# Attention and soft experts in one kernel: another order and pace for the loads of keys, values and expert weights

## The chip, the cores and the metric

The kernel runs on one core of a Trainium2 chip. Times are device microseconds of one execution. Three executions of the kernel before took 250.63, 252.06 and 254.31 us; their median, 252.06 us, is the time before. A fourth execution was taken by the hardware profiler and took 248.69 us; the profile that is quoted below is that one.

## The reference

The kernel computes windowed attention with a linear distance bias, and feeds its output as tokens into a soft mixture of experts. Cut to what matters:

```
# q, k, v: [8 batches, 8 heads, 576, 64]
scores = (q @ k^T) / 8
rel    = pos[:, None] - pos[None, :]
scores = where((rel >= 0) & (rel < 128), scores - slope[h] * |rel|, -1e9)
attn   = exp(scores - rowmax) / (rowsum + 1e-9)
x      = (attn @ v) as [4608 tokens, 512 features]

# phi: [512, 32 slots], w1: [8 experts, 512, 1024], w2: [8 experts, 1024, 512]
logits = x @ phi
d      = softmax of logits over the tokens      # dispatch
slot_input = d^T @ x                            # [32, 512], 4 slots an expert
slot_out[e] = relu(slot_input[e] @ w1[e]) @ w2[e]
c      = softmax of logits over the slots       # combine
out    = c @ slot_out                           # [4608, 512]
```

All inputs and the output are float32. Queries and keys carry a factor of 8, so the scores are well spread.

## The kernel before, in words

**Tiles.** A token tile is 128 queries of one batch with all eight heads. A batch has 576 = 4 x 128 + 64 tokens, so two batches make nine tiles: four of an even batch (t = 0 to 3), then five of the odd batch, whose last (t = 4) holds the two tails of 64 of both. There are 36 tiles, numbered k = 0 to 35; the last batch takes its tiles in the order 1, 2, 3, 4, 0. A tile has two halves (g = 0, 1) of 64 queries each.

**Keys** lie in memory by blocks of 64 keys, nine blocks (0 to 8) a batch, 128 KB each with all heads. They stay in SBUF in a ring of twelve blocks (`keys`, in the tile `kq`); `first_key` says where a batch starts. Half g of tile t reads three blocks from 2(t-1)+g on; t = 0 reads blocks 0 and 1 alone, and t = 4 reads blocks 6 to 8 of both batches. So tile 2 of a batch is the first to read block 5, tile 3 needs blocks 4 to 7, and block 8 is read by t = 4 alone.

**Queries** have two buffers (256 KB a tile, `load_q`); the load for tile k + 2 is asked for after tile k's scores. **Values** (264 KB a tile of 128 keys, `load_v`) have five buffers in the list `v_free`; the tails of two batches have a buffer of their own (`load_v_tails`, 264 KB).

**The pipeline** over k (lines 617 to 671) does, in one pass: VectorE merges the two halves of the window in the scores of tile k (`merge`, L274), adds the bias and takes the row maxima with their signs turned (`rowmax`, L283, into the small tile `nb`, of which there are two buffers, so half g of the next tile writes the buffer of half g of this one); ScalarE takes the exponentials (`expo`, L298); TensorE transposes tile k - 1's exponentials (`flip`, L316), ScalarE copies them to SBUF (`take`, L319), GpSimd cuts the window's corners (`split`, L336 and L339); TensorE forms tile k - 2's weighted values (`values`, L352, and `values_ex`, L364), then tile k + 1's scores (`scores`, L260); VectorE divides by the row sums (`x_store`, L375 to L378); tile k - 3's tokens are transposed (`x_flip`, L384) and copied (`x_keep`, L387). Every four tiles come the logits, the running dispatch maximum and sum, and `slot_sum` (L397 to L460). Each engine runs its instructions in the order in which this text issues them.

**Expert weights** come in 64 units of 512 KB (`units`): 32 of `w1`, then 32 of `w2`. The first NW = 35 go to a ring of 35 tiles; the next 16 go into buffers that the attention no longer needs (`place`: first the keys' and queries' tile, then values, then work areas); the last 13 reuse the ring after the first expert matmuls have read it.

**The pace of the weights.** All of these loads are issued by SyncE (SP), one after another, and each waits on SP until its buffer is free. To keep the units from being asked for too soon, `hold` (L144) first issues a transfer of four bytes from `nb` to a scratch row `beat`: SP cannot issue it before VectorE has written `nb`, and the unit stands behind it. In the text below this transfer is called a note. Before the change, tiles 3 to 29 have one note and one unit each, tiles 30 to 33 one note and two units; the tiles n - 3 = 33 and n - 2 = 34 ask for two more units each after the next tile's scores, and one is asked for after the loop. From there on the units are asked for in the same order with the last steps of the attention.

**The order at the start.** SP asks for key blocks 0 and 1, a small constant, key blocks 2 and 3, value 0, `phi` and a constant; ScalarE's queue asks for query 0, constants and query 1. `loads(0)`, called after tile 0's scores, asks for query 2, value 1 and key blocks 4 and 5; `loads(k)` goes on in that way, and `after_values(k)` loads values into the buffers that tile k was the last to read.

## Time and profile before

| | before |
|---|---|
| median of 3 executions | 252.06 us (250.63 to 254.31) |
| profiled execution | 248.69 us |
| its span, first to last instruction | 247.0 us |
| mean granted TensorE clock | 0.985 |
| TensorE busy | 233.9 us, 95% |
| VectorE, ScalarE busy | 176.3 us, 166.2 us |
| moved by the DMA engines | 72.87 MB, mean 295 GB/s |

The pipeline over the 36 tiles takes the first 185 us or so, the experts and the output the rest. In the profile, a line such as `L260` is a line of the kernel; `SPq` and `ACTq` are the queues of SyncE and ScalarE, on which loads are issued; the duration of an issue is the queue's own time, not the transfer's. In square brackets behind a row stands how long the engine was idle before it, and what ended that. The tile names are the program's: `kq` keys and queries, `va` values, `w` weights, `s` scores, `area` exponentials and their transposes, `nb` the turned maxima, `beat` the target of the notes.

### The profile page before, as it was taken

What the parts mean: (1) busy time and instruction counts of PE and PEld (TensorE: products, weight loads), DVE (VectorE), ACT (ScalarE), POOL (GpSimd) and SP (SyncE); (2) the same over time, 40 slices, a digit from 0 to 9 for tenths busy, and PEclk for the clock granted to TensorE, in tenths of its full rate; (3) what the DMA queues carried; (4) which work ended last, traced back from release to release, by engine and by line L of the source; (5) the groups of instructions that cost most, each with busy time, mean ns of one, the idle gap of its engine ahead of it and who ended that gap; (6) DMA issues with size and microseconds to landing.
All of it is one profiled execution on the core that took longest, in us unless ns stands there. A gap on an engine that the chain in (4) does not pass through costs nothing.

```text
span 247.0 us, 12332 instructions
## 1 busy us (share of the span) xinstructions
PE 233.9 (95%) x4867; PEld 176.4 (71%) x4869; DVE 176.3 (71%) x971; ACT 166.2 (67%) x474; POOL 94.7 (38%) x235
## 2 busy tenths in 40 slices
PE   7799999999999999999999999999998899999982
PEld 3488887877788778787788788788875433866640
DVE  1877878977998898798789899889876411244451
ACT  2778987969788888797797969868954110033441
POOL 2038355724642765086077507557550010000000
PEclk9999999999999999999999999999999999999985
DMA  6979987889889588798778789999878999977997
GB/s 172 305 244 320 302 246 218 248 300 309 241 252 308 178 284 271 248 353 272 253 225 259 258 234 362 354 343 338 293 249 282 416 401 411 409 308 312 353 374 298
DMA packets 28491, 72.87 MB, mean 295 GB/s; under 512 B 3344, under 2 KB 3858, under 8 KB 28434
## 3 DMA queue, kind: packets, MB, share of 16 engines
q1 hardware_dynamic: 27714, 71.25, 83.9%
q10 hardware_dynamic: 720, 0.84, 1.2%
q8 instruction: 38, 0.62, 1.0%
q14 instruction: 19, 0.16, 0.2%
HBM read 62.64 MB, written 9.44 MB: 292 GB/s over the span
## 4 chain that ended last, share of the span: by engine, by line
PE 50%; DVE 5%; issue 1%; ACT 1%; DVEq 0%
PE xp L352 7%; PE s L260 7%; PE op L803 6%; PE hp L767 6%; PE pt L316 5%; PE po L824 5%; PE xq L384 3%; PE xp L364 3%; PE ap L448 2%; PE lp L397 2%; DVE sq L283 1%; DVE xs L378 1%; PE dp L435 1%; DVE s L274 1%; PE ot L816 1%
## 5 line engine op out<-in xcount | busy, mean ns | idle before, releaser
L298 ACT ACTIVATE area<-sq,nb 128x128 f32<-128x128 f32 x288 | 89.5, 400 | 3.4 <-DVE nb L283 2.7
L339 POOL TENSOR_SCALAR_AFFINE_SELECT area<-area 64x256 f32<-64x256 f32 x112 | 46.2, 413 | 82.6 <-ACT area L319 73.9
L283 DVE CUSTOM_DVE_ANT_0 sq<-s,cst 128x128 f32<-128x128 f32 x224 | 51.8, 287 | 7.6
L319 ACT COPY area<-pt 128x512 f32<-128x512 f32 x71 | 41.9, 592 | 19.9 <-PE pt L316 18.4
L260 PE MATMUL s<-kq 64*64 64x192 f32 (+2 forms) x1152 | 51.7, 310 | 1.8 <-DMA kq<-k_t 1.4
L336 POOL TENSOR_SCALAR_AFFINE_SELECT area<-area 64x256 f32<-64x256 f32 x112 | 45.7, 418 | 5.8
L260 PEld LDWEIGHTS s<-kq 64*64 64x64 f32 x1152 | 40.0, 135 | 7.0 <-DVE nb L283 3.9
L316 PE MATMUL pt<-unit_r,area 128*128 128x128 f32 x288 | 44.3, 278 | 0.0
L352 PE MATMUL xp<-va,area 128*64 128x66 f32 x1120 | 40.8, 224 | 1.0 <-DVE xs L378 0.5
L352 PEld LDWEIGHTS xp<-va,area 128*64 128x64 f32 x1120 | 36.0, 137 | 7.0 <-issue 4.3
L316 PEld LDWEIGHTS pt<-unit_r,area 128*128 128x128 f32 x288 | 32.2, 141 | 7.1 <-ACT area L298 4.3
L274 DVE COPY_PREDICATED s<-cst,s 128x256 f32<-128x256 int32 (+1 forms) x73 | 30.6, 419 | 6.1 <-PE s L260 6.1
L378 DVE TENSOR_TENSOR xs<-xp,rs 128x256 f32<-128x256 f32 x70 | 26.5, 419 | 1.2
L387 ACT COPY xs<-xq 128x512 f32<-128x512 f32 (+1 forms) x36 | 21.0, 585 | 5.1 <-PE xq L384 4.8
L384 PE MATMUL xq<-unit_r,xs 128*128 128x128 f32 x144 | 22.5, 278 | 1.7 <-DVE xs L378 0.9
L283 DVE DVE_READ_ACCUMULATOR2_ANT nb<- 128x1 f32 x288 | 23.8, 83 | 0.0
L830 DVE COPY ob<-po 128x384 f32<-128x384 f32 x24 | 12.5, 554 | 13.8 <-PE po L824 13.2
L364 PEld LDWEIGHTS xp<-va,area 64*64 64x64 f32 x896 | 15.7, 133 | 7.5 <-issue 6.4
L830 ACT COPY ob<-po 128x384 f32<-128x384 f32 x24 | 10.5, 481 | 14.0 <-PE po L824 13.9
L364 PE MATMUL xp<-va,area 64*64 64x66 f32 x896 | 19.6, 224 | 0.0
L384 PEld LDWEIGHTS xq<-unit_r,xs 128*128 128x128 f32 x144 | 16.2, 141 | 4.1 <-PE pt L316 2.4
L283 DVE CUSTOM_DVE_ANT_0 sq<-s,fine 128x128 f32<-128x128 f32 x64 | 14.9, 287 | 1.9
(106 smaller groups left out, 230.1 us busy)
## 6 DMA issues: line engine op xcount, KB each, us to landing
w<-w SPq DMA_DIRECT2D x48, 512.0 KB
out<-ob SPq DMA_DIRECT2D x24, 384.0 KB
kq<-q_t SPq DMA_DIRECT2D x34, 256.0 KB
va<-v_n SPq DMA_DIRECT2D x32, 264.0 KB
kq<-k_t SPq DMA_DIRECT2D x24, 256.0 KB
kq<-k_t SPq DMA_DIRECT2D x8, 384.0 KB
kq<-w SPq DMA_DIRECT2D x4, 512.0 KB
area<-w SPq DMA_DIRECT2D x4, 512.0 KB
```

The source lines that it names most:

```text
L260: nc.tensor.matmul(parts[par][half[c], jh, KB * o:WIN], lhsT=qt[rows, j], rhs=keys[rows, i:i + 3 - o, j], start=(t > 0 and jh == 0), stop= ...
L274: nc.vector.copy_predicated(window(k, g, us, 0, KB), bc(mask_le, 1, len(range(4)[us])), window(k, g, us, P, KB))
L283: nc.vector.tensor_tensor_reduce(out=s["sq"][:, u], in0=window(k, g, u, 0, P), in1=bias[:, u] if tiles[k][1] else zero.to_broadcast([P, P] ...
L298: nc.scalar.activation(dst, s["sq"][:, u].rearrange("p (a w) -> p a w", a=2), AF.Exp, bias=s["nb"][:, u:u + 1], scale=-1.0)
L316: nc.tensor.transpose(s["pt"][:, u], s["p4"][:, u], ident)
L319: copy(pas[k % 2][:, g].rearrange("p a j m -> p (a j m)"), st[k, g]["pt"].rearrange("p u w -> p (u w)"))
L336: nc.gpsimd.affine_select(dst, pa, [[0, NPAIR], [-1, KB]], ALU.is_gt, 0.0, base=0, channel_multiplier=1)
L339: nc.gpsimd.affine_select(dst, pa, [[0, NPAIR], [1, KB]], ALU.is_ge, 0.0, base=0, channel_multiplier=-1)
L352: nc.tensor.matmul(x[par][half[g], j], lhsT=pas[k % 2][:, g, par, j], rhs=v[:, par, j], start=(j == 0), stop=(t == 0 and j == NPAIR - 1))
L364: nc.tensor.matmul(x[par][half[g], j], lhsT=pps[k % 2][rows, g, j], rhs=v, start=False, stop=(j == NPAIR - 1))
L378: nc.vector.tensor_tensor(x[:, par], xp[par][:, :, 0:D], bc(rs[:, par], 2, D), op=ALU.mult)
L384: nc.tensor.transpose(st["xq", k][:, P * j:P * j + P], xns[k % NXN][:, P * j:P * j + P], ident)
```

## The change

1. Key blocks 4 and 5 of the first batch are asked for ahead of value 0, not in `loads(0)`.
2. The notes and units start at tile 1 instead of tile 3, with one unit a tile through tile 33. Tiles 33, 34 and 35 ask for two, three and two more after the next tile's scores (in tile 35: after the values), in place of two, two and the one after the loop.
3. In the tiles 1, 2, 15, 28, 29, 30, 32 and 33 the note reads the maxima of the second half instead of the first.
4. Blocks 6 to 8 of a batch, one load of 384 KB at t = 1, become blocks 6 and 7 (256 KB) at t = 1 and block 8 of both batches (128 KB each) at t = 2 of the odd batch.
5. A tile asks for one value load at most: where two buffers come free at once (t = 4 of an odd batch), the second load follows one tile later. The value tails of two batches are asked for at the first tile of the odd batch instead of at t = 0 of the even one.

```diff
-WFIRST = 3
+WFIRST, WLAST = 1, NTT - 2
+TAIL_LOADS = {3: 2, 2: 3, 1: 2}
+LATE = (1, 2, 15, 28, 29, 30, 32, 33)
...
+        load_k(0, 4, 6)
         load_v()
         nc.sync.dma_start(phi, phid)
         nc.sync.dma_start(ends, seld)
...
-        if t == 0 and b < last:
+        if t == 0 and 0 < b < last:
             now.append(k_part(b, 4, 6))
         if t == 1:
-            now.append(k_part(b, 6, NB))
+            now.append(k_part(b, 6, NB - 1))
+        if b % 2 and t == 2:
+            now += [k_part(b - i, NB - 1, NB) for i in range(2)]
...
-        for _ in done:
+        if t or k == 0 or b % 2 == 0:
             load_v()
-        if t == 0 and b % 2 == 0:
+        if b % 2 and t == order(b)[0]:
             load_v_tails(b)
...
     def weights(k):
-        if k >= WFIRST and loaded[0] < NW:
-            hold(st[k, 0]["nb"])
+        if WFIRST <= k < WLAST:
+            hold(st[k, k in LATE]["nb"])
             load_weight()
-            if k >= n - 6:
-                load_weight()
...
+            chain(k, 1)
             weights(k)
-            chain(k, 1)
...
-            if k in (n - 3, n - 2):
-                load_weight()
+            for _ in range(TAIL_LOADS.get(n - k, 0)):
                 load_weight()
...
-        load_weight()
         nc.gpsimd.memset(inp, 0.0)
```

## The prediction

> **What bounds the kernel now.** I read the profile's page first, then the busy time by stretches of the span, then the list of who waited for whom, and last the order in time of TensorE, VectorE, ScalarE and the SyncE queue in the first 20 us. First the page and the stretches; after each pair of times stand its length, then the busy time of TensorE (PE), its weight loads, VectorE (DVE), ScalarE (ACT), GpSimd (POOL), then the granted clock, the busy share of the DMA engines and GB/s.

> ```profile
> span 247.0 us, 12332 instructions
> PE 233.9 (95%) x4867; PEld 176.4 (71%) x4869; DVE 176.3 (71%) x971; ACT 166.2 (67%) x474; POOL 94.7 (38%) x235
> ...
> 10.00:15.00 5.00, 3.61 (x56) 2.97 (x56) 3.49 (x25) 4.25 (x13) 0.00 (x0) 1.00 0.83 274
> 15.00:20.00 5.00, 4.49 (x89) 3.80 (x85) 4.45 (x31) 4.35 (x13) 3.62 (x9) 1.00 0.88 275
> 20.00:150.00 130.00, 128.65 (x2974) 106.17 (x2970) 110.92 (x657) 108.69 (x317) 66.30 (x162) 1.00 0.84 265
> 150.00:172.00 22.00, 21.79 (x511) 18.14 (x508) 19.06 (x112) 18.83 (x57) 14.95 (x37) 1.00 0.99 355
> 172.00:184.00 12.00, 11.52 (x273) 9.54 (x274) 10.30 (x55) 9.34 (x28) 7.38 (x19) 1.00 0.80 277
> 195.00:217.00 22.00, 22.00 (x320) 10.53 (x320) 4.11 (x18) 1.33 (x4) 0.95 (x3) 1.00 1.02 406
> ```

> TensorE sets the pace. From 20 to 172 us it is busy 150.44 of 152 us, so no change in the order of loads can win more than 1.56 us there; from 195 to 217 it never stops. Before the output stage the idle time that loads could have caused is therefore mostly the 1.39 us of 10 to 15 and the 0.51 us of 15 to 20. The transfers are uneven: 406 GB/s is the most that a stretch shows, 355 (share 0.99) is reached from 150 to 172, and 165 to 275 elsewhere.

> Next, single lines of the list of waits, each with the total, the count and the longest:

> ```profile
> PE s L260 <- DMA kq<-k_t: 1.4, 1, 1.4
> SPq L195 <- DMA kq<-q_t: 1.6, 1, 1.6
> SPq L195 <- PE xp L364: 21.2, 16, 2.4
> SPq L178 <- PE pt L316: 36.4, 25, 3.7
> ```

> Only one matmul in the whole span was held up over 1 us by a load: one score matmul by a key load. Every other entry that matters has SP waiting for TensorE, that is, loads waiting for buffers.

> **The change, part by part.** (1) *Key blocks 4 and 5 of the first batch* move from behind query 2 and value 1 to ahead of value 0. The rows below are TensorE around the wait, and SP's issues from the start.

> ```profile
> 9.77 1.09 PE L316 MATMUL pt<-unit_r,area 128*128 128x128 f32 x8
> 12.25 1.53 PE L260 MATMUL s<-kq 64*64 64x192 f32 x32 [1.39 <-DMA kq<-k_t]
> 13.71 1.09 PE L316 MATMUL pt<-unit_r,area 128*128 128x128 f32 x8
> 14.73 1.16 PE L352 MATMUL xp<-va,area 128*64 128x66 f32 x32
> 16.06 1.53 PE L260 MATMUL s<-kq 64*64 64x192 f32 x32 [0.17 <-DVE nb L283]
> ...
> 2.39 0.35 SPq L185 DMA_DIRECT2D kq<-k_t  x1
> 4.38 0.33 SPq L195 DMA_DIRECT2D va<-v_n  x1
> 7.50 0.33 SPq L178 DMA_DIRECT2D kq<-q_t  x1
> 7.87 0.43 SPq L195 DMA_DIRECT2D va<-v_n  x1
> 8.34 0.43 SPq L185 DMA_DIRECT2D kq<-k_t  x1
> 10.74 0.44 SPq L185 DMA_DIRECT2D kq<-k_t  x1
> ```

> The load asked for at 8.34 let tile 2's scores start at 12.25: 3.91 us. SP reached the value load at 4.38 only after 1.6 us of waiting for an earlier transfer (the wait list), so the key load in its place goes out at 4.38, not at 2.8. With 3.91 us it lands at 8.3; with the 5.7 us between the key load of 2.39 and the start of tile 1's scores, it lands at 10.1. Either is ahead of 10.86, when the transposes of 9.77 end. Next late is query 2, asked for at 7.50, now with 256 KB more ahead of it. It came two transfers (520 KB) before the key load that ended the wait.

> ```profile
> 10.00:12.00 2.00, 0.86 (x8) 0.63 (x6) 1.82 (x15) 1.87 (x6) 0.00 (x0) 1.00 1.01 333
> 12.00:14.00 2.00, 1.75 (x35) 1.50 (x36) 0.67 (x4) 1.54 (x5) 0.00 (x0) 1.00 0.87 301
> 14.00:16.00 2.00, 1.89 (x40) 1.59 (x38) 1.81 (x16) 1.84 (x6) 0.03 (x1) 1.00 0.54 165
> ```

> At 333 GB/s those 520 KB are 1.6 us, so query 2 was there by about 10.7; 256 KB more are 0.8 us, so 11.5 at the latest. Tile 2's scores then start at 10.86 to 11.5: 0.75 to 1.39 us earlier.

> That gain does not reach tile 2's end whole, because of ScalarE:

> ```profile
> 10.13 1.28 ACT L298 ACTIVATE area<-sq,nb 128x128 f32<-128x128 f32 x4 [0.55 <-DVE nb L283]
> 11.32 1.04 ACT L319 COPY area<-pt 128x512 f32<-128x512 f32 x2
> 12.26 1.28 ACT L298 ACTIVATE area<-sq,nb 128x128 f32<-128x128 f32 x4
> 14.15 1.28 ACT L298 ACTIVATE area<-sq,nb 128x128 f32<-128x128 f32 x4 [0.62 <-PE pt L316]
> ```

> It works without a break from 10.13 to 13.54 on tile 1, which the change does not touch. The second exponentials, ended at 13.54, release the last four of the eight transposes; now all eight begin at 13.71. With early scores the first four can run before that, and the last four start at 13.71 instead of 13.71 + 1.09 / 2 = 14.26. So 0.55 us remain: the weighted values come at 14.18 and tile 3's scores at 15.51. ScalarE's wait of 0.62 before 14.15 shrinks with it. Tile 3's scores need the load of 10.74: it was there by 16.06 with 384 KB, and is now 256 KB, 0.4 us less at 333 GB/s, so by 15.66 at worst. I take -0.5 us (ends 0 and -1.39; nearer to the ScalarE row, which holds whatever query 2 does). With TensorE full from 20 us on, it stays won to the end.

> (2) *Two more units of weights at the start.* Tiles 1 and 2 now each ask for 512 KB (tile 3 was the first), while 264 KB of value tails go to the next batch and 128 KB of keys to later. That is about 0.65 MB more between 12 and 18 us. From 14 to 16 alone, (406 - 165) GB/s x 2 us = 0.48 MB is free, and from 12 to 14 another 0.2. Cost 0; without that room 0.65 MB at 406 GB/s, 1.6 us, for loads that are used a tile and more later.

> (3) *One unit instead of two in tiles 30 to 33*, with two or three in tiles 33 to 35 after the scores. The stretch from 150 to 172 loses about two units (1 MB of its 7.8); 172 to 184 takes them, where (406 - 277) x 12 us = 1.5 MB is free. At the end of the last tile the count of units is 40 either way, so the saturated stretch from 195 on sees the same queue. TensorE does not wait for a load in either, so 0 in the profiled execution.

> (4) *Eight notes wait for the second maxima.* VectorE around tiles 1 and 2, and SP's first two notes:

> ```profile
> 11.24 0.08 DVE L283 DVE_READ_ACCUMULATOR2_ANT nb<- 128x1 f32 x1
> 13.19 0.43 DVE L274 COPY_PREDICATED s<-cst,s 128x256 f32<-128x256 int32 x1 [1.23 <-PE s L260]
> 14.61 0.42 DVE L274 COPY_PREDICATED s<-cst,s 128x256 f32<-128x256 int32 x1
> 15.39 0.08 DVE L283 DVE_READ_ACCUMULATOR2_ANT nb<- 128x1 f32 x1
> ...
> 19.04 0.66 SPq L144 DMA_DIRECT2D beat<-nb  x1
> 23.55 0.59 SPq L144 DMA_DIRECT2D beat<-nb  x1
> ```

> SP stands some 1.42 us longer there, the distance between the merges of 13.19 and 14.61, which open a tile's first and second maxima. Behind it on SP are the unit, the value load and the next query and key loads. Those value and query loads wait for TensorE anyway, 21.2 / 16 = 1.3 and 36.4 / 25 = 1.5 us each, and are used more than a tile later: 0; without this cover each would go out up to 1.4 us later.

> (5) *Key loads of 256 + 128 KB instead of 384, value tails later, one value load per tile.* Eight more issues of 0.43 us and two more notes of 0.59 on a queue that mostly waits: 0. The last key blocks are asked for two tiles, some 9 us, ahead of their scores, the tails three to four tiles ahead; against 3.9 to 5.7 us from issue to use that is enough.

> [...]

> Sum: 247.0 - 0.5 = 246.5 us of span. The profiled execution took 248.69 (1.69 around the span), so 248.2. The median of the runs, 252.06, is 3.37 above it; the same half microsecond off gives **251.6 us**.

> **The rivals.** *Late keys in the timed runs* (A). The runs are 3.37 us slower than the profiled execution, and something in them waits that the profile does not show. The best candidate is the stretch at share 0.99:

> ```profile
> 147.96 1.14 SPq L185 DMA_DIRECT2D kq<-k_t  x2
> 153.99 0.99 SPq L154 DMA_DIRECT2D w<-w  x2
> 159.05 0.89 SPq L154 DMA_DIRECT2D w<-w  x2
> ...
> 155.58 1.48 PE L260 MATMUL s<-kq 64*64 64x192 f32 x32
> ```

> Two key loads of 147.96 are used at 155.58, and double units stand ahead of later ones. If all 3.37 us are lost there, the change takes them back: 252.06 - 3.37 - 0.5 = 248.2. Against it: the profiled execution shows no wait there.

> *Nothing* (B). Query 2 or tile 3's keys come so late that tile 3's scores stay at 16.06, or the key load, which SP cannot issue before 4.38, queues longer than 5.7 us: 252.1.

> *The notes become a wait* (C), slower. A note reads the minima's buffer, and VectorE may not write that buffer again until the note has landed.

> Tile 1's note can go out at 11.3 (VectorE's rows above); its buffer is written again at 15.39, or 14.3 once the 1.23 us wait is gone: 3.0 us. A note's landing is in no row; the nearest is the 3.91 us key load, so up to 0.9 us of stall. For the notes of tiles 2 and 3, with a unit ahead (512 KB at 333 GB/s, 1.6 us), 5.5 us stand against a tile of 4.5: 1.0 us each. If TensorE follows all three, 2.9 - 0.5 = +2.4, 254.5. It decides from a landing of 3.0 us in tile 1 and 4.5 after. Against: notes at that pitch hold up nothing now, and ScalarE, which comes next, is busy with copies.

> *A fixed cost per transfer* (D). Of the 3.91 us, 256 KB at 406 GB/s are 0.65; if the other 3.3 us kept the engines from other work, eight more loads would cost 26 us: 278. Against: at 3.3 us each, 512 KB units would move at 114 GB/s, and they move at 406 from 195 to 217. [...]

> **How the numbers follow.** Forecast 0.50 (251.6), A 0.15 (248.2 to 251), B 0.20 (252.1), C 0.13 (252.3 to 254.5, seldom more), D 0.02. The range 249.1 to 253.6 leaves out the lower half of A, the upper half of C and D. What a measurement can tell from no change is about 2%, 5.0 us. No case but a full A with more behind it saves that: 0.02; D and a C that goes on past tile 3 lose it: 0.04; within: 0.94.

> **What would show it.** Tile 2's scores starting at 10.9 to 11.5 with a wait under 0.7, ended by a query load; the last transposes of tile 1 still at 13.7; tile 3's scores about 15.5, and everything to the end half a microsecond earlier. The stretch from 150 to 172 falls near 310 GB/s. VectorE waiting for a note in tiles 2 to 4 would be C; a score matmul waiting for keys after tile 3, or a weights wait after 195, would prove (2) or (3) wrong.

## The result and the profile after

| | before | after |
|---|---|---|
| median of 17 executions | 253.95 us (250.15 to 257.98) | 255.26 us (252.24 to 265.39) |
| profiled execution | 248.69 us | 254.91 us |
| its span | 247.0 us | 253.2 us |
| mean granted TensorE clock | 0.985 | 0.982 |

After over before is 1.0117, 95% interval 1.007 to 1.0164. So the change makes the kernel about one per cent slower: less than the 2% that the chances speak of, but slower, where the forecast was half a microsecond faster. The ratios here leave out executions more than 1.5% above the fastest of their kernel; two experiments get none for that reason, and only their median is given. The profiled execution of before, at 248.69 us, is below all 17 timed ones, so the 6.2 us between the two spans are more than the change costs on average.

The page of after, its first lines and the line of one DMA queue (packets, megabytes, share of the time of 16 engines), and the same line of before:

```profile
span 253.2 us, 12347 instructions
PE 234.6 (93%) x4867; PEld 176.7 (70%) x4869; DVE 176.4 (70%) x971; ACT 166.0 (66%) x474; POOL 94.7 (37%) x235
...
q8 instruction: 38, 0.62, 1.1%
```

```profile
q8 instruction: 38, 0.62, 1.0%
```

No engine has more to do than before. TensorE is busy 0.7 us longer, and the span is 6.2 us longer: TensorE stands idle. The stretches of after say where (the columns are those of the prediction):

```profile
20.00:150.00 130.00, 125.94 (x2904) 103.37 (x2900) 107.98 (x636) 105.21 (x307) 64.52 (x158) 1.00 0.85 264
150.00:172.00 22.00, 21.84 (x470) 17.86 (x464) 19.27 (x114) 18.45 (x54) 13.43 (x33) 1.00 0.87 275
172.00:184.00 12.00, 10.55 (x281) 9.21 (x277) 9.99 (x62) 10.79 (x34) 8.36 (x22) 1.00 0.88 293
184.00:195.00 11.00, 9.87 (x172) 7.51 (x176) 5.74 (x20) 3.58 (x9) 1.54 (x4) 0.84 0.84 283
```

From 20 to 150 us TensorE lost 2.71 us more than before (125.94 busy instead of 128.65), from 172 to 184 another 0.97, and from 184 to 195 the granted clock, 1.00 everywhere else here, is 0.84. The list of waits of after names what ended the idle time of the matmuls (total, count, longest):

```profile
PE xp L355 <- issue: 3.2, 2, 2.0
...
PE s L263 <- issue: 1.2, 1, 1.2
...
PE lp L400 <- issue: 0.4, 1, 0.4
```

"issue" is time in which an engine waits for nothing that the profile shows. In order of time, the three longest of these stands are:

```profile
22.93 0.81 PE L355 MATMUL xp<-va,area 128*64 128x66 f32 x20
24.93 0.57 PE L355 MATMUL xp<-va,area 128*64 128x66 f32 x12 [1.19 <-issue]
...
50.81 1.48 PE L263 MATMUL s<-kq 64*64 64x192 f32 x30
53.45 0.54 PE L263 MATMUL s<-kq 64*64 64x192 f32 x2 [1.15 <-issue]
...
181.64 0.92 PE L355 MATMUL xp<-va,area 128*64 128x66 f32 x23
184.56 0.51 PE L355 MATMUL xp<-va,area 128*64 128x66 f32 x9 [2.00 <-issue]
```

Each breaks a run of equal matmuls in the middle: 20 of 32 done, then nothing for 1.19 us, then the other 12. No wait for an operand is on record there. What was missing, by the measurements of the next part, is the instructions.

**How instructions come.** TensorE has 4867 matmuls, 4869 weight loads and some 133 instructions of its sequencer, 9869 in before. The queue marked "instruction", q8, carries 38 packets, each of 16384 bytes in the traces of before and after. Counted along TensorE's stream, every one of these stands lies just ahead of instruction 448 + 256 j: in after at 704, 1216, 1728, 1984, 4032 and 7872, in before at 1984 and 6848 (one or two later in kernels with as many sequencer instructions more). With 38 x 256 = 9728 I take one packet as a block of 256 TensorE instructions. A block's packet follows the moment at which TensorE starts on the block before it, which I call the request; that the packet is asked for there is my reading of the times. It starts 0.2 to 6.5 us behind the request in 477 of 480 blocks of the profiles of this study (in the other three up to 0.4 us ahead of it), lasts 0.9 to 2.8 us, mostly 1.0, and where TensorE has run dry it goes on 1.1 to 1.6 us after the packet's end. In the steady loop 256 instructions last about 5.1 us. So, by my estimate, a packet that starts over 5.1 - 1.0 - 1.4 = 2.7 us behind its request comes too late. From the packets and instructions of after, all in us:

```
request   packet starts      packet ends   TensorE goes on   stand
 19.00    22.64 (+3.64)       23.70         24.93             1.19
 30.02    33.45 (+3.43)       34.42         35.76             0.42
 41.82    44.72 (+2.90)       45.68         47.01             0.10
 47.01    51.02 (+4.01)       51.92         53.45             1.15
 93.11    95.01 (+1.91)       97.24         98.60             0.10
177.68   182.18 (+4.50)      183.14        184.56             2.00
```

**Where the 6.2 us went.** Compared instruction by instruction, after starts the 700th TensorE instruction 0.83 us earlier than before, and the 8200th (at 193.8 us in after) 6.09 us later. On the way it loses 1.36 us around the stand at 24.9, 0.73 at 35.8, 0.36 at 47.0, 0.86 at 53.4 (before has a stand of its own there), 0.45 at 98.6, wins back 0.08, and loses 3.24 around 184.6: -0.83 + 1.36 + 0.73 + 0.36 + 0.86 + 0.45 - 0.08 + 3.24 = 6.09. The losses around the first five stands come to 3.76, the stands themselves to 2.96; what the rest is made of I have not traced. In the last term 2.00 us are the stand itself; behind it the trace shows the granted clock at 0.5 from 186.0 for 3.4 us (1.00 from 184.0 to 186.0), in which eight transposes took 1.97 us, against 1.09 at 12.80; I estimate that this costs up to half of the 3.4, 1.7. The sums of the recorded stands are 4.96 us in after and 0.45 in before, whose two are at 158.9 (0.21) and here:

```profile
50.98 0.54 PE L260 MATMUL s<-kq 64*64 64x192 f32 x3 [0.24 <-issue]
```

**What the late packets have in common.** SP's queue in after, ahead of the requests of 19.00 and 177.68 (`w<-w`, and `kq<-w` late in the span, are units of 512 KB):

```profile
12.03 0.37 SPq L156 DMA_DIRECT2D w<-w  x1
...
15.75 0.38 SPq L156 DMA_DIRECT2D w<-w  x1
...
18.61 0.38 SPq L156 DMA_DIRECT2D w<-w  x1
...
173.29 0.38 SPq L156 DMA_DIRECT2D w<-w  x1
173.73 1.25 SPq L204 DMA_DIRECT2D va<-v_t  x1
175.02 0.91 SPq L156 DMA_DIRECT2D w<-w  x2
176.02 4.88 SPq L156 DMA_DIRECT2D kq<-w  x4
```

These are the places where the change puts units: three by 19.0, where before had its first at 19.74, and five ahead of 177.68 (two of the last four go out by 176.6). For a measure I take the bytes asked for on the load queues whose packets have not started, 1 us after a request: the backlog. At the request of 19.00 it is 1.31 MB (0.73 at before's 19.88), at that of 177.68 it is 1.85 MB (0.49 at before's 174.83). Over the 480 blocks ahead of 186 us, of the two kernels and the 14 experiments below:

| backlog, MB | blocks | mean from request to packet, us | later than 2.7 us |
|---|---|---|---|
| under 0.3 | 87 | 1.27 | 3% |
| 0.3 to 0.6 | 184 | 1.92 | 15% |
| 0.6 to 0.9 | 145 | 2.40 | 38% |
| 0.9 to 1.2 | 41 | 3.15 | 61% |
| 1.2 to 1.6 | 18 | 3.30 | 72% |
| over 1.6 | 5 | 4.07 | 100% |

The correlation is 0.57: delays grow with the backlog, but the backlog does not decide the single case. Before has 1.2 MB behind the requests of 164.77 and 169.78 and gets away with 1.64 and 2.69 us; the longest delay of all, 6.54 us in the experiment keys_only, stands behind 1.1 MB.

### The profile page after: what moved, and what is told of

Same layout as the page of the kernel before. It is cut to its first block, busy times and chain, and to the rows that moved or that the text cites. A ratio compares the mean times of both kernels' runs of the same rounds, so it can differ in the third digit from the quotient of the medians.

```text
span 253.2 us, 12347 instructions
## 1 busy us (share of the span) xinstructions
PE 234.6 (93%) x4867; PEld 176.7 (70%) x4869; DVE 176.4 (70%) x971; ACT 166.0 (66%) x474; POOL 94.7 (37%) x235
## 5 line engine op out<-in xcount | busy, mean ns | idle before, releaser
L263 PE MATMUL s<-kq 64*64 64x192 f32 (+2 forms) x1152 | 51.1, 307 | 2.4 <-issue 1.2
L319 PE MATMUL pt<-unit_r,area 128*128 128x128 f32 x288 | 45.2, 282 | 0.0
L355 PE MATMUL xp<-va,area 128*64 128x66 f32 x1120 | 41.6, 225 | 3.8 <-issue 3.2
L263 PEld LDWEIGHTS s<-kq 64*64 64x64 f32 x1152 | 39.2, 133 | 7.7 <-DVE nb L286 2.0
L319 PEld LDWEIGHTS pt<-unit_r,area 128*128 128x128 f32 x288 | 33.0, 143 | 7.1 <-ACT area L301 4.0
L367 PE MATMUL xp<-va,area 64*64 64x66 f32 x896 | 20.2, 228 | 0.1
```

Of the source, the lines that this page charges most:

```text
L263: nc.tensor.matmul(parts[par][half[c], jh, KB * o:WIN], lhsT=qt[rows, j], rhs=keys[rows, i:i + 3 - o, j], start=(t > 0 and jh == 0), stop= ...
L319: nc.tensor.transpose(s["pt"][:, u], s["p4"][:, u], ident)
L355: nc.tensor.matmul(x[par][half[g], j], lhsT=pas[k % 2][:, g, par, j], rhs=v[:, par, j], start=(j == 0), stop=(t == 0 and j == NPAIR - 1))
L367: nc.tensor.matmul(x[par][half[g], j], lhsT=pps[k % 2][rows, g, j], rhs=v, start=False, stop=(j == NPAIR - 1))
```

## The experiments

My theory after the first comparison was that the new bursts of units delay the instruction blocks. The rivals: that the stands come from the key loads, that they sit at chance places of the stream, and that the notes cost the time.

**Keys alone** (keys_only).

```diff
+        load_k(0, 4, 6)
         load_v()
...
-        if t == 0 and b < last:
+        if t == 0 and 0 < b < last:
```

> The kernel before with part 1 alone: key blocks 4 and 5 asked for ahead of value 0. Theory I (instructions): TensorE gets its instructions in blocks of 256 by transfers of 16 KB on the same DMA engines, and stands at the end of a block when that transfer comes late behind a burst of loads; the changed kernel lost its time there (1.19 us at 24.9, 1.15 at 53.5, 2.00 at 184.6). Without the early units the queue is short at 20 us: tile 3's scores 0.6 to 1.2 us earlier than before, no stand of over 0.7 us at 24 us, ratio 0.990 to 1.000 of before. Theory N (the notes hold VectorE, part 2 and 4): the same, 0.995. Theory O (the prologue order itself costs later): slower, 1.005 or more.

252.74 against 251.63 us, ratio 1.0032 (0.9989 to 1.0075), above the 0.990 to 1.000 that my theory gave. In its profile TensorE runs 0.77 us ahead of before up to 50 us. The stands of after at 24.9 and 184.6 are not there: the first one is 0.65 at 50.6, and the tail has one of 0.25. But there is a longer one, which the profile puts down to ScalarE:

```profile
155.48 0.69 PE L353 MATMUL xp<-va,area 128*64 128x66 f32 x16 [1.63 <-ACT area L299]
```

It lies at a block's end, one behind instruction 448 + 256 x 24, and 1.41 us behind the end of a packet that started 6.54 us after its request. This profile's span is 249.4 us, 2.4 more than that of before. So the early gain of step 1 is there and the two losses at the places of the moved units are not; but late blocks also cost time where the change moved no unit.

**Weights alone** (weights_only).

```diff
-WFIRST = 3
+WFIRST, WLAST = 1, NTT - 2
+TAIL_LOADS = {3: 2, 2: 3, 1: 2}
+LATE = (1, 2, 15, 28, 29, 30, 32, 33)
```

(with `weights` and its calls as in the change, key and value loads as before)

> The kernel before with the new pace of the weights alone (parts 2 and 3: from tile 1, one a tile, the late notes, the new loads in tiles 33 to 35); keys and values as before. Theory I: the bursts at 12 to 20 us and at 173 to 177 us are there, so TensorE stands without a wait at the end of a block near 24 us (0.5 to 1.5 us) and near 183 us (1 to 2 us), and the ratio is 1.005 to 1.02. Theory O (the loss is in the key and value loads): 1.000 or below.

254.95 us, ratio 1.0172 (1.0109 to 1.0236). TensorE's order in its profile has both places again, in the same run of matmuls:

```profile
25.57 0.34 PE L354 MATMUL xp<-va,area 128*64 128x66 f32 x5 [0.72 <-issue]
...
184.90 0.28 PE L354 MATMUL xp<-va,area 128*64 128x66 f32 x2 [3.02 <-issue]
```

Its interval lies above that of keys_only: the loss belongs to the pace of the units, steps 2 to 4 of the prediction together. Which of the three costs how much is not separated by this run.

**One unit for 34** (one_unit). This kernel does not load units 1 to 34.

```diff
     def load_weight():
...
+        if 0 < n < NW:
+            wt[units[n]] = wt[units[0]]
+            return
```

> The changed kernel with 34 of the first 35 units of weights left out: their matmuls read unit 0 instead, so the output is not the reference's; the notes and all else stay. Theory I: with 17.8 MB taken from the queue every transfer of instructions starts within 2.5 us of the block's request, TensorE never stands for more than 0.3 us without a wait before 185 us, and the ratio to the kernel before is 0.96 to 0.985, with a smaller spread between runs. Theory N: the notes are still there, so VectorE still waits and the ratio stays over 1.00.

254.08 us, ratio 1.011 (1.0058 to 1.0163): which was not what was expected. The ring tiles of the units left out are never filled, and the 13 units at the end of the order, which reuse the ring, went out at 17 to 46 us, during the tiles, and made a burst of their own. TensorE around one stand and SP ahead of it:

```profile
52.77 0.36 PE L252 MATMUL s<-ramp 64*64 64x384 bf16 x4 [3.33 <-DVE nb L289]
```

```profile
37.90 2.14 SPq L159 DMA_DIRECT2D w<-w  x3
...
42.44 0.38 SPq L159 DMA_DIRECT2D w<-w  x1
...
44.92 0.96 SPq L159 DMA_DIRECT2D w<-w  x2
```

The packet behind the stand of 3.33 us started 6.11 us after its request. The releaser named is the maxima, which ended inside the stand; by its place in the stream and its packet it is one of the stands above. The stretches of the same kernel:

```profile
20.00:60.00 40.00, 34.22 (x801) 29.02 (x802) 28.37 (x171) 28.66 (x83) 21.09 (x53) 1.00 0.91 323
60.00:150.00 90.00, 88.93 (x2042) 72.44 (x2038) 77.54 (x451) 75.05 (x221) 46.22 (x112) 1.00 0.54 161
```

With the burst (323 GB/s) TensorE loses 5.78 of 40 us, without units (161 GB/s) 1.07 of 90. So the experiment does not show what it was planned for, but it shows something else: where the burst went, the stands went.

**Another place in the stream** (shift). 48 more TensorE instructions at the start, by more and smaller warm-up matmuls, so that each block ends at another matmul.

```diff
-WARM = 7
+WARM = 2
+TINY = 27
...
+        for _ in range(TINY):
+            nc.tensor.matmul(idle_bank[:, 0:8], lhsT=warm[:, 0:P], rhs=warm[:, 0:8], start=True, stop=True)
+        idle_work(2)
```

> The changed kernel with 48 more TensorE instructions in the warm-up at the start (27 tiny matmuls and 3 long ones fewer, in the same 3 us), so that every block of 256 instructions ends 48 instructions, about 1 us, earlier in the tiles; loads and notes are the same. Theory I: the stands of TensorE move by 48 instructions against the tiles and change in number and length; the sum of those over 0.3 us before 185 us (4.8 us in the changed kernel's profile) goes to another value, 1 to 7 us, and the ratio moves with it. Theories N and O: no change against the changed kernel's 1.012 by more than 0.003.

Median 259.16 us (254.84 to 261.49) against 251.63. TensorE's order in the profile, which is of the execution of 261.49 us:

```profile
24.77 0.49 PE L323 MATMUL pt<-unit_r,area 128*128 128x128 f32 x3 [1.37 <-ACT xs L394]
...
162.78 0.60 PE L267 MATMUL s<-kq 64*64 64x192 f32 x4 [3.04 <-issue]
...
191.10 0.27 PE L323 MATMUL pt<-unit_r,area 128*128 128x128 f32 x1 [3.15 <-issue]
```

The stands move to other matmuls (transposes at 24.8 where after has weighted values) and stay at 256-instruction steps. It is the block and not the matmul that stands. The new place was no better: the early and the late stand remain, one of 3.04 at 162.8 is added, and the five stands come to 9.00 us, more than the 1 to 7 that I had expected.

**The tail's units moved out** (tail_spread, spread4, all_late). Two of the tail's units go to tiles 10 and 20, one behind each maxima's note there; the second kernel starts at tile 3 again and has four such tiles; the third, moreover, has all single units wait for the second maxima.

```diff
-TAIL_LOADS = {3: 2, 2: 3, 1: 2}
+TAIL_LOADS = {2: 3, 1: 2}
+EXTRA = (10, 20)
...
+            if k in EXTRA:
+                hold(st[k, 0]["nb"])
+                load_weight()
```

> The changed kernel, but two of the units asked for in tile 33 move to tiles 10 and 20 (each then has one unit behind the first maxima's note and one behind the second's), so that no five units stand in the queue at 173 to 177 us. Theory I: the transfer of instructions asked for near 178 us starts within 2.7 us, TensorE's stand of 2.00 us at 184.6 and the half clock that followed it are gone: 3 us less than the changed kernel, ratio 0.995 to 1.003 of before. If the end of the tiles has another cause: still 1.01.

```diff
-WFIRST, WLAST = 1, NTT - 2
+WFIRST, WLAST = 3, NTT - 2
-EXTRA = (10, 20)
+EXTRA = (8, 14, 20, 26)
```

> As tail_spread, and the units start at tile 3 as before the change, with four tiles (8, 14, 20, 26) of two units. Theory I: the stand of 1.19 us near 24.9 is gone too, the earlier start of tile 3's scores (1.1 us) stays: ratio 0.988 to 0.998. If the early units did no harm: the same as tail_spread.

```diff
-LATE = (1, 2, 15, 28, 29, 30, 32, 33)
+LATE = range(NTT)
```

> As spread4, with the note of every tile behind the second maxima, so that a unit follows the query and key loads 1.4 us later and the bursts are shorter. Theory I: fewer and shorter stands at the ends of the blocks, ratio 0.985 to 0.996. If the burst of one tile does not matter and only the queue over several tiles does: as spread4. Theory N: more notes on the second maxima, VectorE waits more, slower than spread4 by 0.5% or more.

| kernel | median, us | ratio (95%) | profiled execution, us | stands in its profile, us | early | tail |
|---|---|---|---|---|---|---|
| tail_spread | 255.42 | 1.0078 (0.9982 to 1.0173) | 252.83 | 5, sum 3.30 | 1.53 at 26.8 | 0.37 |
| spread4 | 255.76 | 1.0099 (1.0002 to 1.0196) | 260.51 | 10, sum 8.68 | none | 3.02 |
| all_late | 252.76 | 1.0016 (0.9939 to 1.0093) | 252.03 | 7, sum 3.21 | none | 0.62 |

All three ratios lie above what I had forecast for them; only the intervals of tail_spread and all_late reach into it. Without units in tiles 1 and 2 there is no stand ahead of 30 us. Stands in the middle are there instead, and spread4 keeps one of 3.02 us in the tail, with two units less there, behind a packet that started 5.45 us after its request, at a backlog of only 0.8 MB. The three profiled executions lie up to 8 us apart, so their sums do not compare; but this stand is against my theory of the tail, which stays open. all_late speaks against the notes as the cause: it has all of them on the second maxima and is not slower than spread4.

**Half units** (halves, halves_again): spread4 with each ring unit as two loads of 256 KB, one behind each of the tile's two notes.

```diff
+            else:
+                for i in range(2):
+                    hold(st[k, i]["nb"])
+                    half_weight(i)
```

> As spread4, with each unit in two loads of 256 KB, one behind either note of its tile. Theory I: the longest wait of a transfer of instructions falls under 3 us up to 170 us, ratio 0.985 to 0.996. If the fixed cost of a load counts (27 more loads, 27 more notes): slower than spread4.

> The kernel halves again, for a narrower interval. Theory I and the first result: ratio 0.990 to 0.998, the stands under 1.5 us each.

251.49 us, ratio 0.9945 (0.9864 to 1.0025), and timed again 250.21 us, 0.9855 (0.9803 to 0.9907). Compared with spread4 (1.0099) the same bytes go in more and smaller transfers, further apart. The interval of the second measurement lies below spread4's and that of the first still touches it; size and distance changed together, so they are not told apart. In halves packets still started up to 4.55 us after their request, where I had expected under 3.

**Without 47 of the units** (few_units). Units 1 to 34 and the last 13 are not loaded.

```diff
+        if 0 < n < NW or n >= NW + len(place):
+            wt[units[n]] = wt[units[0]]
+            return
```

> The changed kernel with 47 of the 64 units left out (units 1 to 34 and the last 13; their matmuls read unit 0, so the output is not the reference's). Unlike in one_unit no later unit can move forward into the tiles. Theory I: up to 170 us transfers of instructions start within 2 us of the block's request on the mean 1.5 us, no stand over 0.3 us at a block's end before 175 us, the last scores 4 us earlier than in the changed kernel, ratio to before 0.965 to 0.985. Theory N (33 notes are still there) or O: the last scores where they were, ratio near 1.01.

248.73 us (246.80 to 249.18), ratio 0.9797 (0.9741 to 0.9853). The stretch from 20 to 150 us:

```profile
20.00:150.00 130.00, 128.75 (x2990) 106.74 (x2994) 111.85 (x663) 109.69 (x319) 67.22 (x165) 1.00 0.57 168
```

The loads fall to 168 GB/s, the mean delay of a block from 2.2 to 1.23 us, one block of 32 is later than 2.7, and no stand at a block's end is left. This is the cleanest test of the cause: the instructions are the same 38 packets and the 33 notes are kept, only the loads are fewer. The units missing among the experts win nothing there: the last 1700 matmuls and weight loads take 61.4 us here and 61.3 in after. It also bears on the 3.4 us between the median and the profiled execution of before: this kernel's span of 246.8 and its profiled 248.52 agree with its timed executions. That before's timed executions have stands that its profile lacks is therefore likely; no trace of them shows it.

**Paced** (paced): halves, but with no two loads of weights close together: a half unit behind the second maxima's note, a half after the tile's value load, and in eight tiles a third half behind the first maxima's note.

```diff
-EXTRA = (8, 14, 20, 26)
+EXTRA = (5, 9, 13, 16, 19, 22, 25, 28)
...
             if k in EXTRA:
                 hold(st[k, 0]["nb"])
+                half_weight()
+            hold(st[k, 1]["nb"])
+            half_weight()
...
+                if WFIRST <= k < WLAST:
+                    half_weight()
```

> As halves, but the first half of a unit waits for the second maxima's note and the second half follows the value load of its tile; eight tiles have a third half behind the first maxima's note. Theory I: less stands in the queue when a block is asked for: mean delay of the instruction transfers under 2.1 us, sum of the stands under 4 us, ratio 0.985 to 0.998. If halves are enough: as halves, 0.9945. If the keys now come late behind a half: a wait of TensorE for a key load, and slower.

249.80 us (249.05 to 250.36), ratio 0.9852 (0.9801 to 0.9903): faster than both kernels. Two of its stretches, and the only stand:

```profile
20.00:150.00 130.00, 128.26 (x2980) 106.16 (x2978) 111.33 (x659) 109.36 (x319) 67.19 (x165) 1.00 0.88 281
150.00:172.00 22.00, 22.00 (x511) 18.09 (x508) 19.08 (x115) 18.74 (x57) 14.95 (x37) 1.00 0.87 284
```

```profile
179.94 0.45 PE L369 MATMUL xp<-va,area 128*64 128x66 f32 x7 [0.16 <-issue]
```

It moves more than after in these stretches (281 against 264 GB/s), and TensorE is busy 128.26 of 130 us instead of 125.94. So the mean rate is not what hurts. That the bursts are fits this, as spread4 moves the same bytes in larger loads at 1.0099; against halves_again (0.9855) the wider spacing wins nothing more.

**After once more** (after_again), unchanged.

> The changed kernel again, on this chip. Theory I: the stands near 25 us (0.7 to 1.8 us) and near 184 us (over 1 us) come back, since the bursts ahead of them are in the program; the smaller ones between may move or go. Ratio 1.005 to 1.018. If the stands are chance: none at these two places.

255.18 us, ratio 1.0061 (1.001 to 1.0112), span 251.6, six stands with a sum of 4.69. The early and the late one are back at the same two blocks' ends:

```profile
25.16 0.34 PE L355 MATMUL xp<-va,area 128*64 128x66 f32 x5 [1.02 <-issue]
...
183.85 0.33 PE L355 MATMUL xp<-va,area 128*64 128x66 f32 x4 [1.50 <-issue]
```

Those in between, 0.53 at 52.0, 1.05 at 92.9, 0.21 at 138.1 and 0.38 at 161.6, are not all the ones of the first profile: two are the change's, the others vary from one execution to the next.

**The two early units alone** (early_only).

```diff
-WFIRST = 3
+WFIRST = 1
```

(and no unit of its own for tile 33, so that the count is the same)

> The kernel before with one thing changed: notes and units start at tile 1 instead of tile 3 (behind the first maxima); tile 33 then has none of its own. Theory I: a stand of 0.7 to 1.8 us at a block's end between 23 and 27 us, as in the four other kernels with early units and in none without; the tail, now a note and two units lighter, without a stand over 1 us at 177 to 190; ratio 1.002 to 1.010. If the early units do no harm: 0.998 to 1.002 and no such stand.

Median 255.08 us (250.23 to 256.73) against 253.55 (250.86 to 255.88). The four executions, 250.23, 254.41, 255.75 and 256.73 us, do not decide whether this kernel is slower. TensorE's order in the profile, which is of the execution of 255.75 us:

```profile
28.15 0.34 PE L352 MATMUL xp<-va,area 128*64 128x66 f32 x5 [2.09 <-issue]
```

The early stand is there at a backlog of 1.58 MB, the late one is not. Over all 16 profiles, the six with units in tiles 1 and 2 and no load missing have a stand of 0.72 to 2.09 us at 24 to 29 us (after, after_again, weights_only, tail_spread, shift, early_only); the eight that start at tile 3 have none ahead of 30 us.

**Paced, with before's keys and values** (paced_old_keys).

```diff
-        load_k(0, 4, 6)
         load_v()
...
-            now.append(k_part(b, 6, NB - 1))
+            now.append(k_part(b, 6, NB))
```

(and the rest of steps 1 and 5 undone)

> As paced, with keys, values and tails asked for as in the kernel before the change. Theory I with the key load's own 0.5 to 1.1 us: the stands are as few as in paced, tile 2's scores wait 1.2 to 1.4 us for keys again, ratio 0.986 to 0.992, up to 0.5% above paced. If parts 1 and 5 are worth nothing: as paced, 0.985; if they cost: below it.

249.87 us (247.39 to 255.49), ratio 0.9793 (0.9669 to 0.9917); its profile has four stands, with 1.18 at 59.6 and 1.86 in the tail. Its interval holds that of paced, so what steps 1 and 5 are worth by themselves is not decided. Its profile is of an execution of 255.49 us, far above the median. In it the expected wait of tile 2's scores for keys does not come; tile 1's scores are later there (10.32 instead of before's 8.10). That it has a tail stand and paced almost none is not explained.

**All together.** The span less the recorded stands, and less half of the time at the clock of 0.5 between 8 and 200 us, is 246.1 to 248.6 us in all 16 profiles, while the spans go from 246.8 to 259.5. For before and after it is 246.5 both. What sets these profiles apart from each other is the stands and the halved clock behind some of them.

## Why the prediction was wrong, point by point

**The bound.** "TensorE sets the pace" was right. From it I took that a load can only matter through a tile that someone waits for; the list of waits, where a load holds up one matmul over 1 us, seemed to prove it. The page's line of q8 and the list's entries "issue" were both in front of me: TensorE's own instructions come in packets too (q8, 38 of them, which the page of before counts with 1.0% of the time of the 16 engines), and by the estimate above these have to start within 2.7 us.

**(1) Key blocks earlier: the mechanism held, the size was off, to the good side.** TensorE's order in after:

```profile
11.14 1.73 PE L263 MATMUL s<-kq 64*64 64x192 f32 x32 [0.50 <-DMA kq<-q_t]
12.80 1.09 PE L319 MATMUL pt<-unit_r,area 128*128 128x128 f32 x8
13.82 1.16 PE L355 MATMUL xp<-va,area 128*64 128x66 f32 x32
14.91 1.53 PE L263 MATMUL s<-kq 64*64 64x192 f32 x32
```

Tile 2's scores at 11.14, behind a wait of 0.50 for the query load, are what was forecast (10.9 to 11.5, under 0.7). The term that was mis-sized is ScalarE's cap: the eight transposes run as one group from 12.80, the values come at 13.82 instead of 14.18, and the 0.17 us that tile 3's scores waited for maxima are gone, so these start at 14.91, 1.15 us earlier and not 0.55. My 13.71 for the last four transposes was where TensorE had them behind tile 2's scores in before, and not where ScalarE releases them: in after the last of tile 1's exponentials ends at 13.39, and the last four transposes start at 13.29 to 13.62. That the step won more than forecast was luck. 0.83 of it is left when the first stand comes.

**(2) Two early units at a cost of nothing: this step failed.** I looked for room in GB/s averaged over 2 us, and asked when the data would be used. The same stretches of after:

```profile
12.00:14.00 2.00, 2.00 (x33) 1.54 (x31) 1.70 (x10) 2.00 (x8) 0.00 (x0) 1.00 1.02 340
14.00:16.00 2.00, 2.00 (x60) 1.87 (x62) 1.82 (x13) 2.00 (x7) 0.82 (x2) 1.00 0.78 212
16.00:18.00 2.00, 2.00 (x26) 1.55 (x18) 1.86 (x11) 1.62 (x5) 1.78 (x5) 1.00 1.02 375
```

Of the 0.68 MB of room that I had counted from 12 to 16 us, 0.17 were used (340 and 212 GB/s instead of 301 and 165): the second unit went out only at 15.75. From 16 to 18 the engines were full (share 1.02), and at the request of 19.00 the backlog was 1.31 MB, where before has 0.73. The instruction block behind it started 3.64 us after its request: 1.36 us lost, more than step 1 had won. That the stand is this step's is shown by its place, in six profiles of six with early units and in none of eight without; a loss of time by this step alone is not, since the times of early_only do not decide it.

**(3) Units moved to the end of the attention: this step failed more dearly.** The stretch from 150 to 172 did fall (275 GB/s; I had said near 310), and 172 to 184 did take the units (293). But five units and the deferred value tails together, just ahead of one request, made a delay of 4.50 us; with the halved clock behind it, about 3.2 of the 6.1 us. That the change's tail has such a stand in four profiles of four (after, after_again, weights_only, shift: 1.50 to 3.15 us) and before's order has none over 0.3 in two (before, keys_only), nor early_only with two units less there, is shown; that fewer units cure it is not, by spread4 and paced_old_keys.

**(4) The notes**, rival C: VectorE waits for one of them once, 0.5 us in all. Its group for the maxima, the program's `tensor_tensor_reduce` under the profile's name (x count, busy, mean ns, idle time and what ended most of it):

```profile
L286 DVE CUSTOM_DVE_ANT_0 sq<-s,cst 128x128 f32<-128x128 f32 x224 | 51.8, 287 | 8.1 <-DMA beat<-nb 0.5
```

It is 0.49 us at 18.56. So C exists at a fraction of its price. It is not the loss: few_units keeps the notes and has no stand at a block's end.

**(5) More, smaller transfers**: rival D is refuted: halves has 27 more loads than spread4 and is not slower, where D's 3.3 us each would be 89. What else this step does is undecided, except that its later value tails stand in the burst of the tail.

**Rival A** was probably right that something waits in the timed executions that the profile of before does not show, and wrong on what: weights_only, which has one unit instead of two in the tiles 30 to 33 as the change has, takes no 3 us back, but is slower. **The median**: I carried the gap of 3.37 us over unchanged, as if it were a constant; it is likely, though not shown, made of the same stands that the change adds to. What would have proven steps 2 and 3 wrong by my own list, a wait for keys or weights, did not come: I had listed only waits for tiles.

## What to carry to other kernels

Ahead of adding or moving loads, look at where the engine that sets the pace gets its instructions from: the page's "instruction" queue, the stands named "issue", and their distance counted in instructions. In after the list of waits has no matmul that waited for a load from 20 to 185 us, and TensorE still stood 1.19 and 2.00 us there, where a block was requested behind a burst of units; in halves, a few microseconds apart, the same bytes did not slow this kernel (0.9945 and 0.9855 of before). And where timed executions lie several microseconds above the profiled one, ask what varies before carrying the difference over.
